# Loading the first 256 tokens by tile, f32 transposes of the first x, and mask constants ahead of GpSimd's loads in a fused attention and gated-MLP kernel

## Chip, cores and metric

The kernel runs on 1 core of one Trainium2 chip. The metric is the device time of one execution in microseconds (us). Before the change it is 263.32 us, the median of three runs.

## What is computed

Attention over 4 batches, 8 heads, 768 tokens and head width 64, followed by a gated MLP with a gated residual. Heads 0, 2 and 6 are causal; the other five see only the first 4 tokens and a window of 64.

```python
scores = where(mask, q @ k.T / 8, -1e9)          # per batch and head
a = softmax(scores)                              # mask: causal, or causal & (sink | window)
x = (a @ v) -> [3072, 512]                       # heads side by side
ffn = (gelu(x @ w_gate) * (x @ w_val)) @ w_out   # d_ff = 1536
out = x + sigmoid(x @ w_res) * ffn               # float32
```

## The kernel before

The 3072 tokens are cut into six chunks of 512 tokens (`CHUNKS`), that is four tiles of 128. For each chunk the kernel computes attention for four pairs of heads (`PAIRS`: 0 and 2, 4 and 6, 1 and 3, 5 and 7), and then the MLP. Chunk 0 is computed in two halves of two tiles, here called first and second half, so that its first gate and value products (`g0` to `g3`, `v0` to `v3`, `L1135`) can start on the first half.

Every operation is a task of a graph. Nothing is scheduled while the program is built. `PLAN` is a list of task numbers written out by hand (a `w` entry puts that many matmuls on a blank tile on TensorE as fillers, and a suffix such as `a` or `d` picks ScalarE or VectorE for a task that may run on several engines). Each engine runs its tasks strictly in the order of the list. `PLACES` gives the buffer for each allocation. `assign_waits` adds the semaphore waits that the dependencies need. A task number is its position in the order of construction, so any added or removed task renumbers the list.

The steps that the change and the prediction touch:

- `loads_first` (`L640`) loads the first 256 tokens of queries and keys of batch 0 as f32: four transfers on the SP queue for keys and four on the ACT queue for queries, one per pair of heads (`ldf`, `L651`). Each is followed by a cast to f16 on VectorE, ScalarE or GpSimd (`c16`, `L657`, `L658`), by transposes on TensorE (`qkT`, `L666`) and by a copy out of PSUM (`qkE`, `L676`). The transposed keys and queries are `kT` and `qT`. The staging buffers come from `P_st` (three of them) and the f16 copies from `P_x16`.
- The remaining loads are issued by GpSimd (`dma`, `L538`), which casts to f16 on the way: queries and keys in `loads_rows` (transposed at `L723`, copied out at `L734`), values in `values`, and weights in `load_weights`. GpSimd also builds the identity and the masks (`L512` to `L525`, tasks named `const`); in `PLAN` these stand between its first loads.
- `scores` (`L892`) multiplies keys by queries, the exponentials follow on ScalarE (`L908`, `L912`), and the masks are applied on VectorE (`L944`). `sink_scores` (`L983`) does the four sink tokens.
- `weigh` multiplies by the values (`win`, `av`, `avk`), takes the reciprocal of the sums (`L1070`), and writes x twice in chunk 0: as f16 for the transposes (`norm16`, `L1081`) and as f32 for the residual (`norm`, `L1083`).
- `to_features` transposes the f16 x on TensorE (`xT`, `L1105`) and copies it out of PSUM (`xE`, `L1113`).
- `gate_value` does the gate and value products, the gelu (`L1140`, `L1171`) and their product (`L1143`, `L1173`). Exponentials and gelu need different activation tables on ScalarE.

In `mm` (`L473`) a matmul may be issued as one full product (`L476`) or as two products of 64 columns of the array (`L477`), whichever tiling TensorE is in when the task comes up.

Of the kernel before, what the change touches and what calls it, by code (L numbers as in the profile page):

```python
# [4 lines left out]
NHEAD = 8  # L5
# [8 lines left out]
NPAIR = NHEAD // 2  # L14
# [415 lines left out]
def build_kernel(nc, q, k, v, w_gate, w_val, w_out, w_res, out):  # L430
# [105 lines left out]
    def dma(eng, prio, cost, out_ap, in_ap, bufs=(), deps=(), name="ld", grp=None):  # L536
        issue = 0.85 if eng == "pool" else 1.2
        return G.add(eng, issue, lambda e: e.dma_start(out_ap(), in_ap), deps, prio, bufs=bufs, dma=cost, name=name, grp=grp)  # L538
# [1016 lines left out]
```

## Time and profile before

| what | value |
|---|---|
| median of three runs | 263.32 us (262.81 to 264.11) |
| the profiled execution | 263.6 us, span 261.9 us |
| TensorE clock granted, mean | 1.000 |
| TensorE busy | 251.9 us, 96% of the span |
| VectorE busy | 206.2 us, 79% |
| ScalarE busy | 159.1 us, 61% |
| GpSimd busy | 104.3 us, 40% |
| moved by DMA | 33.70 MB, mean 129 GB/s |

The profile describes one execution. Its engines are PE (TensorE matmul), PEld (TensorE weight load, beside PE), DVE (VectorE), ACT (ScalarE), POOL (GpSimd) and SP (SyncE). A group row names line, engine, operation, output and inputs, shapes and count, then busy time in us and the mean ns of one, and behind the bar the engine's idle time ahead of it with what ended it. A row of the timeline begins with start and length in us. The chain of waits is followed backwards from the last instruction, at each step to what released it.

### The profile page before, as it was taken

The numbers are of one execution on the slowest core, as the hardware profiler recorded it, in microseconds if no ns is written. First come the engines' busy times: TensorE is split into PE (matmuls) and PEld (weight loads), VectorE is DVE, ScalarE is ACT, GpSimd is POOL, SyncE is SP. The second block draws the span as 40 slices with busy tenths as digits, with TensorE's granted clock in tenths as the row PEclk, the third lists the DMA queues.
The fourth block names the chain that finished last, engine by engine and source line by source line (L and its number), as shares of the span: only waits on it lengthen the run. The fifth ranks groups of instructions, "written<-read, shape, count | busy, mean of one in ns | idle before, by whom it ended". The sixth has DMA issues, their size and how long they took to land.

```text
span 261.9 us, 8050 instructions
## 1 busy us (share of the span) xinstructions
PE 251.9 (96%) x3404; PEld 179.7 (69%) x3404; DVE 206.2 (79%) x472; ACT 159.1 (61%) x282; POOL 104.3 (40%) x142
## 2 busy tenths in 40 slices
PE   6899999999999999999999999999999999999992
PEld 4467754457567667666687567689678678987891
DVE  3599645799879898498998587999587898577975
ACT  2489535867574997245894347884546994555420
POOL 8699952505809906168371563002201010110031
PEclk9999999999999999999999999999999999999999
DMA  6999999996999997999998799609975017230013
GB/s 152 175 175 206 195 202 192 195 148 104 151 174 207 217 120 116 141 205 162 164 103 119 107 149 261 95 3 93 247 105 82 4 12 113 36 49 3 0 36 130
DMA packets 102131, 33.70 MB, mean 129 GB/s; under 512 B 86736, under 2 KB 97232, under 8 KB 102096
## 3 DMA queue, kind: packets, MB, share of 16 engines
q0 software_dynamic: 72592, 18.36, 79.2%
q1 hardware_dynamic: 27840, 13.52, 25.5%
q10 hardware_dynamic: 1664, 1.31, 1.5%
q8 instruction: 27, 0.44, 0.8%
q14 instruction: 8, 0.07, 0.1%
HBM read 29.36 MB, written 10.49 MB: 152 GB/s over the span
## 4 chain that ended last, share of the span: by engine, by line
PE 88%; DVE 7%; DMA 2%; issue 1%; ACTq 1%; ACT 0%; DVEq 0%
PE ps L476 47%; PE ps L477 31%; PE ps L892 5%; DMA qks<-in_q_dram 2%; PE ps L1105 1%; PE ps L1016 1%; DVE x L1081 1%; PE ps L983 1%; DVE xtok L1083 1%; PE ps L1456 1%; ACTq L651 1%; DVE otile L1397 1%; DVE hT L1270 0%; DVE kT L734 0%; PE ps L666 0%
## 5 line engine op out<-in xcount | busy, mean ns | idle before, releaser
L1401 POOL DMA_DIRECT2D out_dram<-otile x16 | 14.5, 904 | 95.7 <-DVE otile L1397 63.5
L476 PE MATMUL ps<-xT,wg 128*128 128x512 f16 (+1 forms) x172 | 38.5, 337 | 0.4 <-DVE x L1081 0.4
L476 PE MATMUL ps<-xT,wv 128*128 128x512 f16 (+1 forms) x168 | 37.5, 339 | 0.0
L1171 ACT ACTIVATE gact<-ps 128x512 f16<-128x512 f32 x38 | 21.8, 596 | 23.6 <-PE ps L476 13.8
L1173 DVE SCALAR_TENSOR_TENSOR hT<-gact,ps 128x512 f16<-128x512 f16 x38 | 26.0, 683 | 11.4 <-PE ps L476 4.9
L538 POOL DMA_DIRECT2D qks<-in_k_dram x35 | 28.8, 842 | 15.1 <-PE ps L723 8.2
L538 POOL DMA_DIRECT2D qks<-in_q_dram x35 | 30.2, 902 | 7.8 <-DMA qT<-qks 7.8
L1245 DVE TENSOR_TENSOR ps<-ps,otile 128x256 f32<-128x256 f32 x60 | 24.3, 428 | 8.9 <-PE ps L477 4.1
L538 POOL DMA_DIRECT2D va<-in_v_dram x24 | 24.3, 1021 | 12.4 <-PE ps L476 12.4
L476 PEld LDWEIGHTS ps<-xT,wv 128*128 128x128 f16 x168 | 16.1, 98 | 11.2 <-ACT gact L1263 0.2
L476 PEld LDWEIGHTS ps<-xT,wg 128*128 128x128 f16 x172 | 16.3, 98 | 10.1 <-DVE x L1081 0.7
L1263 ACT ACTIVATE gact<-ps 128x512 f16<-128x512 f32 x30 | 16.7, 597 | 10.7 <-PE ps L477 5.5
L908 ACT ACTIVATE ea<-ps 128x1024 f16<-128x1024 f32 (+2 forms) x24 | 21.5, 923 | 1.4 <-PE ps L892 1.4
L1270 DVE SCALAR_TENSOR_TENSOR hT<-gact,ps 128x512 f16<-128x512 f16 x30 | 19.5, 683 | 2.2 <-PE ps L476 1.2
L1341 ACT ACTIVATE srs<-ps 128x512 f32<-128x512 f32 x22 | 12.9, 599 | 12.3 <-PE ps L477 8.6
L1241 ACT ACTIVATE ps<-ps 128x256 f32<-128x256 f32 x25 | 9.3, 371 | 16.2 <-PE ps L476 11.8
L1373 DVE TENSOR_TENSOR otile<-otile,ps 128x256 f32<-128x256 f32 x33 | 13.7, 418 | 6.5 <-PE ps L477 4.3
L477 PE MATMUL ps<-xT,wv 128*64 128x512 f16 (+1 forms) x152 | 18.5, 340 | 0.0
L476 PE MATMUL ps<-wo,hT 128*128 128x256 f16 (+1 forms) x114 | 18.2, 295 | 0.0
L477 PE MATMUL ps<-xT,wg 128*64 128x512 f16 (+1 forms) x144 | 17.9, 344 | 0.0
L892 PE MATMUL ps<-qT,kT 64*128 64x64 f16 (+4 forms) x391 | 17.1, 216 | 0.8 <-DVE kT L734 0.5
L1083 DVE TENSOR_TENSOR xtok<-ps,rcp 128x512 f32<-128x512 f32 (+1 forms) x28 | 17.0, 610 | 0.5
(182 smaller groups left out, 594.5 us busy)
## 6 DMA issues: line engine op xcount, KB each, us to landing
out_dram<-xtok SPq DMA_DIRECT2D x4, 1024.0 KB, 6.2
out_dram<-otile POOLq DMA_DIRECT2D x16, 256.0 KB, 4.3
va<-in_v_dram POOLq DMA_DIRECT2D x24, 128.0 KB, 8.2
qks<-in_q_dram POOLq DMA_DIRECT2D x32, 64.0 KB, 7.3
qks<-in_k_dram POOLq DMA_DIRECT2D x32, 64.0 KB, 7.4
wg<-in_moe_w_gate_dram POOLq DMA_DIRECT2D x3, 512.0 KB, 10.6
wv<-in_moe_w_val_dram POOLq DMA_DIRECT2D x3, 512.0 KB, 12.4
wo<-in_moe_w_out_dram POOLq DMA_DIRECT2D x4, 384.0 KB, 21.5
```

Of the source, the lines that this page charges most:

```text
L476: return e.matmul(o, lhsT=lhsT, rhs=rhs, **k)
L477: return [e.matmul(o[h:h + 64], lhsT=lhsT[:, h:h + 64], rhs=rhs, **k) for h in (0, 64)][-1]
L538: return G.add(eng, issue, lambda e: e.dma_start(out_ap(), in_ap), deps, prio, bufs=bufs, dma=cost, name=name, grp=grp)
L892: return [e.matmul(at(scr)[:, oo:oo + w], lhsT=side(BB, qb, low, 1)[half, k0:k0 + 128], rhs=side(BB, qb, low, 0)[half, qq:qq + w], start=T ...
L908: return e.activation(out=o, in_=i_, func=AF.Exp, scale=SM_SCALE)
L1083: t2 = G.add("dve", c_dve(2 * n * 64), lambda e: e.tensor_tensor(out=xview(), in0=avv(0, DHEAD), in1=scale(), op=ALU.mult), [t1] + xdeps, ...
L1171: ta = G.add("act", c_act(512), (lambda gb=gb, ga=ga, gw=gw: lambda e: e.activation(out=at(ga)[:, :], in_=at(gb)[:, gw], func=AF.Gelu))(), ...
L1173: th = G.add("dve", c_dve(512), (lambda vb=vb, ga=ga, f=f, vw=vw: lambda e: e.scalar_tensor_tensor(out=hv(f), in0=at(ga)[:, :], scalar=0.5 ...
L1245: return G.add("dve", c_dve(256), lambda e: e.tensor_tensor(out=at(ps)[:, o], in0=at(ps)[:, BL], in1=at(es)[:, 0:256], op=ALU.add), deps, ...
L1263: ta = G.add("act", c_act(512), (lambda x=x, ga=ga, both=both: lambda e: e.activation(out=two(at(ga)[:, :]), in_=both(x), func=AF.Gelu))() ...
L1270: th = G.add("dve", c_dve(512), (lambda x=x, f=f, ga=ga, both=both: lambda e: e.scalar_tensor_tensor(out=two(hv(f)), in0=two(at(ga)[:, :]) ...
L1401: t = G.add("pool", 1.0, (lambda ot=ot, r0=r0: lambda e: e.dma_start(out[r0:r0 + 128, :], at(ot)[:, :], accum_op=ALU.add))(), ends + [stor ...
```

## The change

- `loads_first` issues two transfers per hardware queue instead of four. Each covers all eight heads of one tile of 128 tokens. The eight casts now belong to halves of a tile (four heads each), and each of the four transpose groups takes one tile of keys or queries with all pairs. The copy out of PSUM writes consecutive tokens.
- In the first half of chunk 0, x is no longer written as f16. The transposes read the f32 x with an f32 identity, `ident32`, which is kept in `xs3` until that buffer's own first use. The copy out of PSUM reads f32 there.
- In the second half of chunk 0, heads 0, 2 and 4, 6 write the f32 x first and cast it to f16 from there; in the new list the cast is on GpSimd. The other two pairs write f16 and f32 as before.
- Every GpSimd load depends on all of GpSimd's constant tasks.
- Copies of the window mask may run on ScalarE too.
- `PLAN` and `PLACES` are replaced for the whole kernel. In the new list the load of ScalarE's exponential table stands right behind its two transfers, there are 33 fillers instead of 42, and one exponential of chunk 1 stands between gelus of chunk 0.

```diff
+    ident32 = xs3[:, 0, :].bitcast(FP32)
...
+    t_ident32 = G.flex({"dve": (0.2, lambda e: e.tensor_copy(out=ident32[:, :], in_=ident[:, :])),
+                        "act": (0.3, lambda e: e.activation(out=ident32[:, :], in_=ident[:, :], func=AF.Copy))}, [t_ident], -58, name="ident")
+    xs3_last = [t_ident32]
...
-        return G.add(eng, issue, lambda e: e.dma_start(out_ap(), in_ap), deps, prio, bufs=bufs, dma=cost, name=name, grp=grp)
+        return G.add(eng, issue, lambda e: e.dma_start(out_ap(), in_ap), list(deps) + (consts if eng == "pool" else []), prio,
+                     bufs=bufs, dma=cost, name=name, grp=grp)
...
+    consts = [x for x in G.tasks if x.name == "const"]
...
-        for p in ORDER:
-            h = PAIRS[p][0]
+        for i in range(2):
             for j, src, eng in ((1, k, "sp"), (0, q, "act")):
-                    view(j, p).rearrange("p (x w) -> p x w", x=2),
-                    src[b, h:h + 3:2, lo:lo + 256, :].rearrange("x (p i) d -> p x (i d)", i=2)))(),
-                    [], -60, bufs=[st[j]], dma=0.5, name="ldf")
+                    view(j, i, 0, 2).rearrange("p (h d) -> p h d", h=NHEAD),
+                    src[b, :, lo + 128 * i:lo + 128 * i + 128, :].rearrange("h p d -> p h d")))(),
+                    [], -60, bufs=[st[j]], dma=0.9, name="ldf")
+                for o in range(2):
...
-        for k_ in (0, 2):
-            ps_ = sorted(ORDER[k_:k_ + 2])
+        for i in range(2):
             for j in (1, 0):
...
-                x16 = Buf(P_x16)
+                x16 = None if c == 0 and l0 == 0 else Buf(P_x16)
...
-        direct = c == 0 or heads[0] % 2
+        direct = x16 is not None and heads[0] % 2
...
-        if not direct:
+        if x16 is None:
+            xdeps.append(t2)
+        elif not direct:
...
+            on = ("dve", "act") if c else ("dve", "act", "pool")
...
+        plain = x16 is None
+        view = (lambda s: at(s)) if plain else at16
...
+            out=at(scr)[:, i * 128:(i + 1) * 128], in_=at(xbuf)[:, l0 + i, cb * 128:(cb + 1) * 128], identity=ident32[:, :])
```

More of the change, by code (lines that the diff above doesn't have):

```diff
@@ L525, in build_kernel @@
         (64, aff(m_win[:, 2, 0:64], ALU.is_ge, 0.0, 0, [[1, 64]], -1))])
-    t_win0 = [spread(("dve",), -50, m_win[:, 3:5, :], m_win[:, 1:2, :].to_broadcast([128, 2, 128]), 256, t_win)]
-    t_win = t_win0 + [spread(("dve",), 600, m_win[:, 5:7, :], m_win[:, 1:2, :].to_broadcast([128, 2, 128]), 256, t_win),
-                      spread(("dve",), 600, m_win[:, 0, :], m_win[:, 1, :], 128, t_win)]
+    t_win0 = [spread(("dve", "act"), -50, m_win[:, 3:5, :], m_win[:, 1:2, :].to_broadcast([128, 2, 128]), 256, t_win)]
+    t_win = t_win0 + [spread(("dve", "act"), 600, m_win[:, 5:7, :], m_win[:, 1:2, :].to_broadcast([128, 2, 128]), 256, t_win),
+                      spread(("dve", "act"), 600, m_win[:, 0, :], m_win[:, 1, :], 128, t_win)]
     for i, vk in enumerate(P_vk.items):
@@ L645, in loads_first @@
         st, half = [Buf(P_st), Buf(P_st)], [Buf(P_x16), Buf(P_x16)]
-        view = lambda j, p: at(st[j])[:, :].bitcast(FP32)[:, p * 256:(p + 1) * 256]
-        h16 = lambda j, p: at(half[j]).rearrange("p c i k -> p (c i k)")[:, p * 256:(p + 1) * 256]
-        for p in ORDER:
-            h = PAIRS[p][0]
+        view = lambda j, i, o, n=1: at(st[j])[:, :].bitcast(FP32)[:, (i * 2 + o) * 256:(i * 2 + o + n) * 256]
+        h16 = lambda j, i, o, n=1: at(half[j]).rearrange("p c i k -> p (c i k)")[:, (i * 2 + o) * 256:(i * 2 + o + n) * 256]
@@ L650, in loads_first @@
+        for i in range(2):
             for j, src, eng in ((1, k, "sp"), (0, q, "act")):
-                ld = G.add(eng, 0.6, (lambda src=src, j=j, p=p, h=h: lambda e: e.dma_start(
-                    view(j, p).rearrange("p (x w) -> p x w", x=2),
-                    src[b, h:h + 3:2, lo:lo + 256, :].rearrange("x (p i) d -> p x (i d)", i=2)))(),
-                    [], -60, bufs=[st[j]], dma=0.5, name="ldf")
-                def cast(on, j=j, p=p):
-                    return lambda e: (e.activation(out=h16(j, p), in_=view(j, p), func=AF.Copy) if on == "act" else
-                                      e.tensor_copy(out=h16(j, p), in_=view(j, p)))
@@ L659, in loads_first @@
-                tok[j, p] = G.flex({e: (0.4, cast(e)) for e in ("dve", "act", "pool")}, [ld], -205, bufs=[st[j], half[j]], name="c16")
-        for k_ in (0, 2):
-            ps_ = sorted(ORDER[k_:k_ + 2])
+                ld = G.add(eng, 0.6, (lambda src=src, j=j, i=i: lambda e: e.dma_start(
+                    view(j, i, 0, 2).rearrange("p (h d) -> p h d", h=NHEAD),
+                    src[b, :, lo + 128 * i:lo + 128 * i + 128, :].rearrange("h p d -> p h d")))(),
+                    [], -60, bufs=[st[j]], dma=0.9, name="ldf")
@@ L662, in loads_first, with cast @@
+                for o in range(2):
+                    def cast(on, j=j, o=o, i=i):
+                        return lambda e: (e.activation(out=h16(j, i, o), in_=view(j, i, o), func=AF.Copy) if on == "act" else
+                                          e.tensor_copy(out=h16(j, i, o), in_=view(j, i, o)))
+                    tok[j, i, o] = G.flex({e: (0.4, cast(e)) for e in ("dve", "act", "pool")}, [ld], -205, bufs=[st[j], half[j]], name="c16")
+        for i in range(2):
             for j in (1, 0):
@@ L663, in loads_first @@
                 scr = Buf(P_ps, "scr0")
-                to, o0 = (BB.kt, lo) if j else (qb, qo)
-                tt = G.add("pe", 0.3, (lambda scr=scr, j=j, ps_=ps_: lambda e: [
-                    e.transpose(out=at16(scr)[64 * x:64 * x + 64, (m * 2 + i) * 128:(m * 2 + i + 1) * 128],
-                                in_=h16(j, p)[:, x * 128 + i * 64:x * 128 + i * 64 + 64], identity=ident[:, :])
-                    for m, p in enumerate(ps_) for i in range(2) for x in range(2)])(),
-                    [t_ident] + [tok[j, p] for p in ps_], 40 * k_ - 205, bufs=[half[j], scr], name="qkT")
+                to, o0 = (BB.kt, lo + 128 * i) if j else (qb, qo + 128 * i)
@@ L670, in loads_first, with ev @@
+                tt = G.add("pe", 0.3, (lambda scr=scr, j=j, i=i: lambda e: [
+                    e.transpose(out=at16(scr)[64 * x:64 * x + 64, p * 128:(p + 1) * 128],
+                                in_=h16(j, i, 0, 2)[:, PAIRS[p][x] * 64:PAIRS[p][x] * 64 + 64], identity=ident[:, :])
+                    for p in range(NPAIR) for x in range(2)])(),
+                    [t_ident] + [tok[j, i, o] for o in range(2)], 80 * i - 205, bufs=[half[j], scr], name="qkT")
                 tt.mode = "col"
-                def ev(on, scr=scr, to=to, o0=o0, ps_=ps_):
+                def ev(on, scr=scr, to=to, o0=o0):
@@ L673, in fn @@
                     def fn(e):
-                        o = at(to)[:, ps_[0]:ps_[1] + 1:ps_[1] - ps_[0], o0:o0 + 256].rearrange("c m (p i) -> c m p i", i=2)
-                        i_ = at16(scr)[:, 0:512].rearrange("c (m i p) -> c m p i", m=2, i=2)
+                        o = at(to)[:, :, o0:o0 + 128]
+                        i_ = at16(scr)[:, 0:512].rearrange("c (m w) -> c m w", m=NPAIR)
                         return e.tensor_copy(out=o, in_=i_) if on == "dve" else e.activation(out=o, in_=i_, func=AF.Copy)
@@ L677, in ev @@
                     return fn
-                t = G.flex({"dve": (c_dve(512), ev("dve")), "act": (c_act(512), ev("act"))}, [tt], 40 * k_ - 205,
+                t = G.flex({"dve": (c_dve(512), ev("dve")), "act": (c_act(512), ev("act"))}, [tt], 80 * i - 205,
                            bufs=[scr, to], name="qkE")
-                for p in ps_:
-                    for i in range(a, a + 2):
-                        (BB.ktok if j else BB.qtok)[p, i] = t
+                for p in range(NPAIR):
+                    (BB.ktok if j else BB.qtok)[p, a + i] = t
@@ L852, in attention @@
                   for cb in (P.heads[0] // 2, P.heads[1] // 2):
-                    to_features(c, cb, P.pr, x16, xdeps, xtbuf, xttoks, l0, len(tiles))
+                    to_features(c, cb, P.pr, x16, xdeps, xtbuf, xttoks, l0, len(tiles), xbuf)
         return last
@@ L1090, in cast @@
                                   e.tensor_copy(out=at(x16)[:, :, 0:n, half], in_=xview()))
-            xdeps.append(G.flex({"dve": (0.57, cast("dve")), "act": (c_act(n * 128), cast("act"))},
+            on = ("dve", "act") if c else ("dve", "act", "pool")
+            xdeps.append(G.flex({e: (0.57 if e == "dve" else c_act(n * 128), cast(e)) for e in on},
                                 [t2], pr + 122, bufs=[xbuf, x16], name="x16"))
@@ L1101, in to_features_dma, with to_features @@
         xttoks += [(cb, t), (cb + 1, t)]
-    def to_features(c, cb, pr, x16, xdeps, xtbuf, xttoks, l0, n):
+    def to_features(c, cb, pr, x16, xdeps, xtbuf, xttoks, l0, n, xbuf):
         scr = Buf(P_ps, "scr")
-        tp = G.add("pe", c_mm(128, n), lambda e: [e.transpose(
+        plain = x16 is None
+        view = (lambda s: at(s)) if plain else at16
+        tp = G.add("pe", c_mm(128, n), (lambda e: [e.transpose(
+            out=at(scr)[:, i * 128:(i + 1) * 128], in_=at(xbuf)[:, l0 + i, cb * 128:(cb + 1) * 128], identity=ident32[:, :])
+            for i in range(n)]) if plain else lambda e: [e.transpose(
             out=at16(scr)[h:h + w, i * 128:(i + 1) * 128], in_=at(x16)[:, cb % 2, i, h:h + w], identity=ident[:, :])
             for i in range(n) for h, w in (((0, 64), (64, 64)) if G.run == "col" else ((0, 128),))],
-            xdeps + [t_ident], pr - 3, bufs=[x16, scr], name="xT")
+            xdeps + [t_ident32 if plain else t_ident], pr - 3, bufs=[xbuf if plain else x16, scr], name="xT")
         ph(c, "xT").append(tp)
+        if plain:
+            xs3_last.append(tp)
         def ev(on):
             def fn(e):
-                o, i_ = at(xtbuf)[:, cb, l0 * 128:(l0 + n) * 128], at16(scr)[:, 0:n * 128]
+                o, i_ = at(xtbuf)[:, cb, l0 * 128:(l0 + n) * 128], view(scr)[:, 0:n * 128]
                 return e.activation(out=o, in_=i_, func=AF.Copy) if on == "act" else e.tensor_copy(out=o, in_=i_)
@@ L1276, in fast @@
         toks[FA:] = toks[FA::2] + toks[FA + 1::2]
-    gvtok, gas, gv_tail, xs3_last = {}, {}, [], []
+    gvtok, gas, gv_tail = {}, {}, []
     def sums(c, h, htoks, pa=0):
```

152 rows, old and new, of tables (PLACES, PLAN) are left out of this document.

## The prediction

> **What bounds the kernel now.** I read the page first, then the chain of waits in order of time, then busy time by stretch, then the rows of the first 30 us. The page:
>
> ```profile
> span 261.9 us, 8050 instructions
> PE 251.9 (96%) x3404; PEld 179.7 (69%) x3404; DVE 206.2 (79%) x472; ACT 159.1 (61%) x282; POOL 104.3 (40%) x142
> PE 88%; DVE 7%; DMA 2%; issue 1%; ACTq 1%; ACT 0%; DVEq 0%
> ```
>
> TensorE is busy throughout, but the 96% hold fillers on `blank`. The chain (start, length, what) shows where PE truly is the bound:
>
> ```profile
> 2.39 6.09 DMA qks<-in_q_dram
> 8.50 0.30 DVE x L658
> 8.85 1.07 PE ps L666 x16
> ...
> 20.89 0.03 issue
> ...
> 26.53 0.43 DVE x L1081
> ...
> 27.64 0.22 PE ps L1105 x4
> 27.87 15.63 PE ps L476 x96
> ...
> 258.40 0.69 DVE otile L1407
> ```
>
> The last query transfer holds the start until 8.50, VectorE and its neighbours until 26.96, and from 27.87 the matrix engine. What reaches 27.87 earlier moves everything behind it. Busy time in those stretches (length; PE, PEld, DVE, ACT, POOL; clock; DMA share; GB/s):
>
> ```profile
> 11.90:27.10 15.20, 13.91 (x269) 9.86 (x268) 13.21 (x43) 13.79 (x26) 15.03 (x22) 1.00 1.47 191
> 27.80:43.50 15.70, 15.70 (x100) 9.13 (x99) 7.50 (x19) 6.65 (x14) 8.48 (x11) 1.00 1.55 194
> 43.50:204.00 160.50, 160.50 (x2008) 111.42 (x2010) 135.24 (x298) 104.46 (x183) 64.02 (x81) 1.00 1.28 144
> ```
>
> In the first row DVE (13.21) and ACT (13.79 of 15.20) are both nearly full. In the others PE never pauses and both have room.
>
> **The change, part by part.** The two transfers per hardware queue carry the same 1.05 MB, but in pieces of one 64-value row (256 B, 4,096 of them) instead of two rows (512 B, 2,048). The rows are: 3.0 to 4.5 us, hardware transfers almost alone; then 9 to 12 us, GpSimd's transfers alone, all small.
>
> ```profile
> DMA packets 863, 0.41 MB, mean 276 GB/s; under 512 B 55, under 2 KB 863, under 8 KB 863
> q0 software_dynamic: 3, 0.00, 0.5%
> DMA packets 2937, 0.49 MB, mean 163 GB/s; under 512 B 2937, under 2 KB 2937, under 8 KB 2937
> ```
>
> The first is 575 packets per us, the second 979. No row has 256-byte packets on the hardware queues. Bounds, from data beginning at 2.39: unchanged bytes per us (276 GB/s) 3.8 us, so 6.2; 979 packets per us 4.2 us, so 6.6; 575 packets per us 7.1 us, so 9.5. I take 979, whose packets are small as the new ones are, and 0.3 us to be seen: last arrival 6.9 against 8.50.
>
> The Trainium skill ("DMA: Bandwidth & Descriptors", Specifications) says transfers below 512 B miss line rate; its section "Why small descriptors are slow" counts 3 extra cycles per packet, 11 for 256 B and 19 for 512 B, so 1.16 times the time per byte. That estimate would put the arrival at 6.8; the bare rule alone speaks against this change, and no run here has shown either.
>
> That nothing else is on the DMA engines meanwhile comes from the constants. GpSimd now does all nine before its first load. In 0 to 12 us it was busy 9.17, of which its DMA issues were 6.75:
>
> ```profile
> 0.00:12.00 12.00, 6.75 (x8) 1.00 1.26 162
> sum 12.00, PE 8.64 PEld 5.38 DVE 5.90 ACT 3.41 POOL 9.17; mean PE 8.64 PEld 5.38 DVE 5.90 ACT 3.41 POOL 9.17
> 1.67 1.11 POOL L538 DMA_DIRECT2D qks<-in_q_dram  x1
> 9.26 0.88 POOL L538 DMA_DIRECT2D qks<-in_k_dram  x1 [2.08 <-DVE x L658]
> 14.63 0.75 POOL L538 DMA_DIRECT2D wg<-in_moe_w_gate_dram  x1
> 24.48 0.61 PE L476 MATMUL ps<-xT,wg 128*128 128x256 f16 x4
> ```
>
> So the constants cost at most 2.4 us: the first load goes from 1.67 to about 3.2. Three packets by 4.5 us say that its data began some 1.7 us after its issue ended at 2.78; now that is about 6.0, when the hardware transfers are nearly done. The later loads wait for nothing that was early. In the new order the first gate weights are GpSimd's eighth load (tenth before), after seven issues of about 0.9 from 3.2, so near 9.5 instead of 14.63, while their first user ran at 24.48. The rows of chunk 1 that are put behind the weights are first needed after 43 us (the chain's piece from 27.87 ends at 43.50, in front of their transposes). Cover gone, each load would cost its issue, 0.9.
>
> From arrival to scores: ACT's table load leaves the path (its new place is ahead of the data).
>
> ```profile
> 2.91 1.28 ACT L657 ACT_TABLE_LOAD   x1 [2.91 <-issue]
> L657 ACT ACTIVATE x<-qks 128x256 f16<-128x256 f32 x2 | 0.8, 416 | 1.2 <-DMA qks<-in_k_dram 1.2
> L676 DVE COPY qT<-ps 128x512 f16<-128x512 f16 x2 | 1.4, 692 | 0.8 <-PE ps L666 0.8
> 11.25 0.40 PE L892 MATMUL ps<-qT,kT 64*128 64x64 f16 x8
> 14.22 0.41 PE L723 MATMUL ps<-ident,qks 128*64 128x128 f16 x8
> ```
>
> It gains nothing on the path, because the last arrival was later. Three ACT casts of 0.42 now follow the last arrival in a row: 6.9 to 8.2; transposes (half of L666's 1.07) 8.7; two evictions of 0.69 on DVE behind each other, partly overlapped: scores at 9.9. By tile, every score needs all four transfers, where pair 0 used to start after half; that early start is lost (the chain does not pass through it). Two score groups and a transpose group (0.40, as much, and 0.41) precede DVE's next eviction: 11.1.
>
> DVE's stretch from there to the last f16 write of x that the transposes wait for, by kinds:
>
> ```profile
> L1081 DVE TENSOR_TENSOR x<-ps,rcp 128x256 f16<-128x256 f32 x8 | 3.3, 420 | 0.1
> L1070 DVE RECIPROCAL rcp<-ps 128x4 f32<-128x4 f32 x8 | 1.4, 175 | 0.0
> L734 DVE COPY kT<-ps 128x512 f16<-128x512 f16 x2 | 1.3, 662 | 0.0
> L734 ACT ACTIVATE qT<-ps 128x1024 f16<-128x1024 f16 x1 | 1.0, 1005 | 0.0
> L1113 ACT ACTIVATE xT<-ps 128x256 f16<-128x256 f16 x1 | 0.4, 377 | 0.0
> L616 DVE COPY vs<-va 64x455 f16<-64x455 f16 (+1 forms) x2 | 1.0, 476 | 0.1
> sum 15.20, DVE 3.65; mean DVE 3.65
> ```
>
> The last row is the ten masks alone. New list: 3 evictions 2.0, masks 3.65, 3 value copies 1.4, 8 reciprocals 1.4, 8 x writes at 0.42 3.4, one x eviction from f32 0.42 (as a 256-wide f32 read), one 1024-wide eviction of chunk 1 that ACT did before 1.3: 13.6 in 34 instructions, with 0.03 between two (as the chain's issue piece at 20.89): 14.6, so 25.7. Six f16 writes of x are gone (2.5), but a 1024-wide eviction, a value copy and one f32 write moved in, so DVE's stretch barely shrinks; it was 11.93 to 26.96. ACT gives up two 1024-wide evictions (1.0 each) and takes 7 instead of 2 x evictions (0.38 each), so it stays beside DVE.
>
> Second half: heads 0, 2 and 4, 6 get their f16 x by a GpSimd cast, behind the residual weights' issue. GpSimd's nearest prices are 0.43 (a 128x256 f16 select) and 0.86 (L1407, 128x256 f32 add).
>
> ```profile
> L496 POOL TENSOR_SCALAR_AFFINE_SELECT m_win<-m_win 128x256 f16<-128x256 f16 x2 | 0.9, 430 | 0.1
> L1407 POOL TENSOR_TENSOR otile<-otile,xtok x4: 722/861/1265, 252.7 to 256.2; 128x256 f32<-128x256 f32 x3, 128x512 f32<-128x512 f32 x1
> L1105 PE MATMUL ps<-ident,x 128*128 128x128 f16 x12 | 1.3, 219 | 0.2 <-DVE xtok L1083 0.2
> L1456 PE MATMUL ps<-blank 128*128 128x256 f16 x25 | 4.7, 326 | 0.0
> 29.04 1.48 PE L476 MATMUL ps<-xT,wg 128*128 128x256 f16 x12
> ```
>
> The second cast may start at about 25.2 and, at 0.6, ends at 25.8, level with DVE; at 0.86 it costs 0.3 to 0.5. Queued behind it are one chunk-1 load and the output weights: no one needs them before 43 us. So the last two transposes run at 25.8 and end at 26.2 (0.39 as at 27.48), against 27.87: 1.7 earlier. By then PE has also done one more value group (4 matmuls, (1.48-0.27)/11 = 0.11 each): 0.44.
>
> f32 transposes: eight of the first half, 0.10 apart as f16 (0.40 for four). No row has one. Bounds: 0, or four times, 8 x 0.30 = 2.4 us, cushioned by fillers (4.7 us of them in the first row's stretch, about half left now). I take 0.4 on the path, nearer the free end because PE waits for DVE there.
>
> Later stages: the new order has PE change its tiling 61 times behind this point, 63 before; one exp stands between gelus in chunk 0, two more table loads in ACT's 9 us of slack (27.8 to 43.5). Taken as nothing; without that cover 2 x 1.28. The tail keeps its order but for two output issues that go from ACT's queue to SP's. Spreads and initial fills that move between engines: nothing, they lie in idle time.
>
> Sum on the profiled execution: 1.7 + 0.44 - 0.4 = 1.7. It took 263.6 (span 261.9), 0.3 over the median 263.32. 263.3 - 1.7 = 261.6.
>
> **The rivals.**
> 1. Small packets hold the start: 575 packets per us, last arrival 9.5 or later, since GpSimd's data then shares the engines from 6.0. Everything shifts by 2.6 against the sum: 263.3 - 1.7 + 2.6, 264.2, and with half of it 262.9. For: 256 B is new on these queues; against: 979 per us of GpSimd's small ones. By the skill's bare 512 B rule this is what happens.
> 2. The change does not do what it says for the end: DVE's stretch hardly shrinks, so with f32 transposes at four times, half covered (1.2 instead of the 0.4 taken), and the cast at 0.86 (0.4) the gain is 1.7 - 0.8 - 0.4 = 0.5: 262.8, no change. For: DVE and ACT both full in the first row. Against: fillers.
> 3. Slower: exp between the gelus. ACT then spends 1.28 + 0.6 + 1.28 = 3.2 in which no gate bank is freed, and PE runs out of PSUM banks. It decides once over 1.7 of the 3.2 is uncovered; wholly uncovered, 263.3 - 1.7 + 3.2 = 264.8. Against: ACT's 6.65 busy of 15.70, and PE has other banks for some 2 us.
>
> **How the numbers follow.** 0.5%, 1.3 us, is about what a measurement tells from no change. My forecast (faster, own range 260.2 to 262.0) 0.55; rivals 1 and 2 0.15 each, mostly within 0.5%; rival 3 or rival 1 at its worst 0.15. Faster 0.57, same 0.28, slower 0.15. The range reaches from arrival at 6.2 with free f32 transposes and 0.8 more found in the order (259.8) to rival 1 at its end (264.2).
>
> **What would show it.** Last first-stage cast before 8.5; scores near 9.9; gate matmuls continuous from about 26; no GpSimd packet before 5 us. Wrong if the last arrival is past 8.5, if the f32 transposes stand over 0.2 apart with PE waited for, if PE pauses between 27 and 35 us, or if the stretch behind it grows.

## The result, and the profile after

The changed kernel takes 260.44 us (median; 260.23 to 261.0), the kernel before in the same series 263.29. The ratio is 0.989, with an interval from 0.986 to 0.992: faster by about 2.85 us, where 1.7 were forecast. The profiled execution took 261.0 us, its span is 259.3. It is the longest of the four; the others took 260.23 to 260.50.

From the page of the changed kernel, the span, the busy times and the shares of the chain of waits:

```profile
span 259.3 us, 8020 instructions
PE 250.1 (96%) x3393; PEld 176.1 (68%) x3393; DVE 203.0 (78%) x453; ACT 164.9 (64%) x298; POOL 105.1 (41%) x144
PE 93%; DVE 2%; DMA 2%; ACT 1%; issue 1%; DVEq 0%
```

The chain had 7% on VectorE and now has 2%. Its rows in order of time (start, length, what):

```profile
0.81 4.67 DMA qks<-in_q_dram
...
5.50 0.46 DVE x L663
...
6.01 0.49 DVE vk L535
...
8.95 0.61 ACT kT L680
...
11.47 0.65 PE ps L895 x13
...
20.02 0.96 ACT vs L622
...
25.57 0.45 PE ps L1115 x8
...
27.23 17.85 PE ps L477 x100
...
255.71 0.69 DVE otile L1419
```

The chain leaves the transfers at 5.5, with the first query tile, and not at 8.50 with the last queries; but scores (L895) run at 11.4. Before, a first group ran at 7.3 and the next at 11.25. From there the chain goes through TensorE and a few ScalarE pieces around 20 us. Between 7.7 and 252 us it has no piece of VectorE, which it followed up to 26.96 before. Busy time in the stretches shown of before (length; PE, PEld, DVE, ACT, POOL; clock; DMA share; GB/s):

```profile
11.90:27.10 15.20, 14.55 (x259) 10.48 (x254) 12.52 (x37) 13.63 (x30) 9.84 (x17) 1.00 1.39 200
27.80:43.50 15.70, 15.70 (x90) 8.53 (x89) 5.80 (x12) 9.68 (x17) 6.32 (x8) 1.00 1.50 196
43.50:204.00 160.50, 160.50 (x2068) 111.19 (x2068) 135.15 (x293) 109.92 (x193) 70.73 (x89) 1.00 1.32 143
```

In the first row VectorE has six instructions fewer (37 for 43) and GpSimd 5.2 us less. In the other two TensorE is full, as before, but it gets through the rest sooner. To see this, I count from the last x transposes of each chunk and add up the planner's own costs of the TensorE work that the list still holds behind that place ("left"). At equal work left, the changed kernel is ahead by 1.35 us at the end of chunk 0's first stage, by 1.3 to 1.4 after chunks 1 to 3, by 1.7 after chunk 4, 2.6 after chunk 5, and 2.7 at the end. By this count half of the gain is in the first 26 us and half comes later. The costs are the planner's estimates, and the first figure is not exact: with the same start, `a_then_b` below ran those transposes at 24.6 in its profiled execution and not at 25.4, because TensorE worked at half rate for a shorter time there (last section).

### The profile page after: what moved, and what is told of

Same layout as the page of the kernel before. It is cut to its first block, busy times and chain, and to the rows that moved or that the text cites. A ratio compares the mean times of both kernels' runs of the same rounds, so it can differ in the third digit from the quotient of the medians.

```text
span 259.3 us, 8020 instructions
## 1 busy us (share of the span) xinstructions
PE 250.1 (96%) x3393; PEld 176.1 (68%) x3393; DVE 203.0 (78%) x453; ACT 164.9 (64%) x298; POOL 105.1 (41%) x144
## 4 chain that ended last, share of the span: by engine, by line
PE 93%; DVE 2%; DMA 2%; ACT 1%; issue 1%; DVEq 0%
PE ps L477 49%; PE ps L478 31%; PE ps L895 6%; DMA qks<-in_q_dram 2%; PE ps L1019 2%; PE ps L726 1%; PE ps L1115 1%; PE ps L1468 1%; PE ps L986 1%; PE ps L670 1%; DVE otile L1409 1%; DVE x L663 0%; DVE vk L535 0%; ACT vs L622 0%; ACT es L911 0%
## 5 line engine op out<-in xcount | busy, mean ns | idle before, releaser
L1413 POOL DMA_DIRECT2D out_dram<-otile x16 | 15.4, 995 | 84.9 <-DVE otile L1409 54.7
L542 POOL DMA_DIRECT2D qks<-in_q_dram x35 | 32.5, 950 | 17.5 <-issue 8.6
L542 POOL DMA_DIRECT2D qks<-in_k_dram x35 | 32.8, 973 | 12.8 <-PE ps L726 12.8
L1257 DVE TENSOR_TENSOR ps<-ps,otile 128x256 f32<-128x256 f32 x60 | 24.9, 431 | 9.8 <-PE ps L478 5.1
L542 POOL DMA_DIRECT2D va<-in_v_dram x24 | 24.1, 1035 | 5.1 <-PE ps L477 5.1
L1353 ACT ACTIVATE srs<-ps 128x512 f32<-128x512 f32 x22 | 13.1, 596 | 15.3 <-PE ps L478 11.6
L478 PE MATMUL ps<-xT,wv 128*64 128x512 f16 (+1 forms) x156 | 19.2, 341 | 0.0
L895 PE MATMUL ps<-qT,kT 64*128 64x64 f16 (+3 forms) x391 | 16.9, 216 | 0.6 <-ACT xT L1125 0.6
L478 PE MATMUL ps<-xT,wg 128*64 128x512 f16 (+1 forms) x144 | 17.3, 344 | 0.0
```

What stands on the lines that cost most here:

```text
L478: return [e.matmul(o[h:h + 64], lhsT=lhsT[:, h:h + 64], rhs=rhs, **k) for h in (0, 64)][-1]
L895: return [e.matmul(at(scr)[:, oo:oo + w], lhsT=side(BB, qb, low, 1)[half, k0:k0 + 128], rhs=side(BB, qb, low, 0)[half, qq:qq + w], start=T ...
L1257: return G.add("dve", c_dve(256), lambda e: e.tensor_tensor(out=at(ps)[:, o], in0=at(ps)[:, BL], in1=at(es)[:, 0:256], op=ALU.add), deps, ...
L1413: t = G.add("pool", 1.0, (lambda ot=ot, r0=r0: lambda e: e.dma_start(out[r0:r0 + 128, :], at(ot)[:, :], accum_op=ALU.add))(), ends + [stor ...
```

## The experiments

Two theories. A: the gain is the start's, from the earlier arrival, as the prediction has it. B: half belongs to the order of the later list. Further: which of the start's edits is it? All ratios are against the kernel before, run beside each kernel (its medians 263.16 to 263.53).

| kernel | median, us | ratio, interval |
|---|---|---|
| a_then_b | 264.99 | 1.007, 1.005 to 1.009 |
| b_then_a | 265.71 | 1.009, 1.006 to 1.012 |
| a_vzero | 259.44 | 0.986, 0.984 to 0.988 |
| a_nofill | 261.38 | 0.993, 0.991 to 0.996 |
| after_again | 260.24 | 0.989, 0.986 to 0.991 |
| a_between | 259.82 | 0.987, 0.984 to 0.989 |
| a_f16x | 262.63 | 0.997, 0.994 to 1.000 |
| a_both | 259.52 | 0.986, 0.983 to 0.988 |
| a_loads8 | 260.56 | 0.990, 0.988 to 0.993 |
| a_best | 259.60 | 0.986, 0.982 to 0.989 |
| a_late_b | 266.57 | 1.014, 1.010 to 1.018 |
| a_row512 | 260.68 | 0.991, 0.989 to 0.994 |

**Start and later order apart: a_then_b and b_then_a.**

```diff
a_then_b (changed kernel's code)
-PLAN = after
+PLAN = after[:245] + (the rest, in the order of before)
b_then_a (code of before)
-PLAN = before
+PLAN = before[:285] + (the rest, in the order of after)
```

> The changed kernel's start (its list up to the end of chunk 0's attention, about 27 us) followed by the old order for everything behind it. Theory: of the 2.8 us gained, the start gave 1.35 (equal TensorE work is reached that much earlier at 27 us) and the later order 1.3. Then this runs at 263.3 - 1.35 = 261.9. Rival: the whole gain comes from the start; then 260.5, as the changed kernel. A third reading, all from the later order: 263.3.

> The mirror: the old start up to the end of chunk 0's attention, then the changed kernel's order. Theory (1.35 from the start, 1.3 from the later order): 263.3 - 1.3 = 262.0. Rival (all from the start): 263.3. Third reading (all from the later order): 260.5.

Both totals are slower than either parent, and no theory's number was met: each seam makes stalls of its own. The chain of a_then_b and then that of b_then_a, near the seam:

```profile
47.14 0.60 ACT srs L1440
47.75 1.28 ACT L912
49.05 1.02 ACT ea L912
50.07 0.60 ACT ek L994
```

```profile
42.01 1.08 ACT gact L1172 x2
...
43.76 1.28 ACT L1459
45.06 0.21 ACT scratch L1459
45.26 0.92 ACT ea L909
```

ScalarE gets table loads and exponentials in front of what TensorE waits for. Behind the seam the two can still be used. Time from chunk 1's last x transposes to the last VectorE addition, and planned TensorE work left at the first:

| | list behind | from, to | time | work left | over the plan |
|---|---|---|---|---|---|
| before | old | 67.6, 258.4 | 190.8 | 181.55 | 9.25 |
| a_then_b | old | 68.0, 259.3 | 191.3 | 181.55 | 9.75 |
| after | new | 65.3, 255.7 | 190.4 | 182.41 | 8.0 |
| b_then_a | new | 70.2, 260.7 | 190.5 | 182.41 | 8.1 |

The new list takes 1.2 to 1.7 us less for the same work, with either start. In plain time it is 0.4 to 0.8; the other 0.86 is the planner's price for the work that the new list still has left there. Part of it shows in the trace. What TensorE waited for between 67 and 257 us, in the kernel before:

```profile
PE ps L477 <- issue: 0.4, 1, 0.4
PE ps L892 <- DVE hT L1270: 0.3, 1, 0.3
```

a_then_b has the wait for hT again (0.3), another of 0.4 for a transfer and one of 0.2, which may be the joint's; the changed kernel and b_then_a have none. Output matmuls in half tiles from 67 us on (groups by line: count | busy, mean ns | idle), in before and after:

```profile
L477 PE MATMUL ps<-wo,hT 128*64 128x256 f16 x216 | 15.5, 274 | 0.4 <-issue 0.4
```
```profile
L478 PE MATMUL ps<-wo,hT 128*64 128x256 f16 x216 | 14.7, 274 | 0.0
```

The same 216 matmuls take 0.8 us less; in a_then_b and b_then_a they take 15.2 and 14.6. Not every group gains: the value products in half tiles take 13.6 us for 96 before and 14.5 for 100 after. So B holds for about half of the gain by the planner's sums, and not by the totals of the two spliced kernels. Which exchange in the list does it is not shown.

**Where in the later list: a_late_b.**

```diff
-PLAN = after
+PLAN = after[:1248] + (the rest, in the order of before)
```

> The changed kernel up to its 1,248th place of the order (about 181 us, just behind the last x transposes of chunk 4), then the rest in the order of the kernel before. Theory 'most of what the later order gained lies in chunks 4 and 5': behind that point the kernel before took 74.6 us for 71.5 of planned TensorE work and the changed kernel 73.8 for 71.7, so the time rises by about 1.0, to 261.2 (ratio 0.992), with TensorE pauses of 0.3 each near 205 and 221 as in the kernel before. Rival 'the gain is spread over all chunks or belongs to the start': it rises by less than 0.4, to at most 260.7 (0.990). The seam itself may add up to some tenths, which would show as a pause right behind 181 us.

This one tells nothing on the question. It is 6.3 us slower, and its chain shows a mishap of the joint:

```profile
214.33 4.32 DMA out_dram<-otile
218.67 0.44 DVE otile L1380
219.15 3.05 PE ps L479 x50
```

An output tile is needed again before its transfer to memory is through, so TensorE stands for 2.8 us. The place of the later gain inside the list stays open.

**The two memsets: a_vzero.** VectorE clears the sink values (L535) between two first casts, from 6.01 to 7.05.

```diff
 PLAN = "0 17 18 214 217 211 1 220 199 212a 216 6 7
-15 218a 16 2 215 ... 9 10 222 5 227 221a 228 229 230 11 12 232
+218a 2 215 ... 9 10 222 5 227 221a 228 229 230 11 12 15 16 232
```

> The changed kernel with VectorE's two initial fills of vk (0.49 us each, now between its first and second cast) moved behind its last eviction of the first 256 tokens, where it idles 1.7 us. Theory: they lie on the chain to the first scores, so scores start 1.0 us earlier (10.4 instead of 11.40) and the kernel takes 259.5 to 260.0 instead of 260.5. Rival: the last key transfer, first cast at 7.25, and the five fillers set the first scores anyway; then no change, 260.5.

It is 0.8 to 1.0 us faster than the changed kernel. In its trace the memsets stand behind the evictions, the first scores come 0.9 earlier, and the second half's x transposes start at 24.1 instead of 25.4. Part of these 1.3 us is not the edit's: TensorE worked at half rate until about 11.6 us in this execution and until about 13.9 in the changed kernel's. a_best below, with the same memsets and half rate until about 13.8, has the transposes at 24.8:

```profile
10.01 1.04 DVE L536 MEMSET vk<- 128x520 f16 x2
10.47 0.45 PEld L896 LDWEIGHTS ps<-qT,kT 64*128 64x128 f16 x15 [0.41 <-issue]
```

**The idle matmuls: a_nofill and a_both.**

```diff
 PLAN = "... 215 8 w20 225 219a ...
-... 224a w5 420 ... w3 431 ... w2 467 ... w3 440 ...
+... 224a 420 ... 431 ... 467 ... 440 ...
(a_both: this and the edit of a_vzero)
```

> The changed kernel without the 13 fillers behind the first transposes (the first 20 stay). Theory: the five ahead of the first scores and the eight later ones stand on TensorE's own chain (1.18, 0.61, 0.33 and 0.43 us pieces of it), and about 0.6 us of that comes back: 259.9. Rival A: they only fill waits, 260.5. Rival B: without them the granted clock falls in this stretch, and it is slower, over 261.

> The changed kernel with the two memsets of the sink values moved behind the last eviction of the first queries and without the thirteen idle matmuls on the blank tile that stand in TensorE's queue after the first loads. With the memsets moved alone the kernel took 259.4 us, without the idle matmuls alone 261.4. Theory 'the five idle matmuls before the first scores now delay them' (they ended at 10.5 where the last eviction had ended at 9.8): first scores at 9.9 instead of 10.5, last transposes of x near 23.6, time near 258.9 (ratio 0.984). Rival 'the idle matmuls pay for themselves, whatever they cost at the start': about 0.9 above the kernel with the memsets moved, as between the other two, 260.3 (ratio 0.989).

Without the 13 later ones the changed kernel takes 0.9 us more (the intervals just overlap), yet with the memsets moved it makes no difference (259.52 and 259.44). a_both starts its scores at 10.00 instead of 10.47 and ends the first stage no earlier (x transposes at 24.0, against 24.1). Neither theory of a_both met its number. a_nofill's 261.38 lies where rival B put it. Its granted clock speaks against B: 0.999 in the profiled execution, and 0.997 in a run of 262.2 against 0.980 in one of 260.4. The matmuls of the profiled execution speak for B. The same six scores in a_nofill and in the changed kernel:

```profile
16.31 0.60 PE L895 MATMUL ps<-qT,kT 64*128 64x128 f16 x6
```
```profile
16.41 0.39 PE L895 MATMUL ps<-qT,kT 64*128 64x128 f16 x6
```

In a_nofill TensorE works at half rate until about 19 us, in the changed kernel and in a_both until about 13.9, all with a recorded clock of 1.00. Whether the missing idle matmuls bring this, and whether it makes the 0.9 in the other runs, is not shown: a_both lacks them too.

**The constants: a_between.**

```diff
-list(deps) + (consts if eng == "pool" else [])
+list(deps)
 PLAN: "4 232 231 233 234 236 235 5", GpSimd's loads, back between the constants as in before
```

> The changed kernel with GpSimd's constants put back between its first loads, in the order in which the kernel before had them, and nothing else of the change undone. Theory 'constants ahead made the start earlier': GpSimd's transfers then share the engines with the first loads of queries and keys from about 3 us on, the last of these lands near 8.3 instead of about 7.0, the last first-stage cast ends near 10 instead of 9.5, and the time rises by about 0.9 to 1.3 us to 261.3 to 261.7 (ratio 0.993 to 0.994). Rival 'the arrival did not decide, VectorE's queue behind it did' (two memsets of 0.49 us and the casts): the last load lands later but the last cast does not move by more than 0.3, and the time stays within 0.4 of 260.4 (0.988 to 0.991).

Neither number is met. The load does not land later, which the rival had expected too, and the time falls by 0.4 us (within the intervals), just below the rival's range. GpSimd's first load is issued at 1.69, as in before:

```profile
1.69 1.10 POOL L543 DMA_DIRECT2D qks<-in_q_dram  x1
...
7.18 1.38 ACT L663 ACTIVATE x<-qks 128x256 f16<-128x256 f32 x4 [3.60 <-DMA qks<-in_k_dram]
...
8.84 0.28 DVE L664 CAST x<-qks 128x256 f16<-128x256 f32 x1
```

The keys' second transfer still lands at 7.1. The last first-stage cast ends at 9.1, earlier than the changed kernel's 9.5. GpSimd's packets do not come before 6 us here either. So with two long transfers on each hardware queue the place of the constants does not move the arrival.

**What moved the arrival: a_loads8 and a_row512.** First four transfers of half the heads, then two transfers with 512-byte pieces:

```diff
a_loads8
+                for o in range(2):
-                    view(j, i, 0, 2).rearrange("p (h d) -> p h d", h=NHEAD),
-                    src[b, :, lo + 128 * i:lo + 128 * i + 128, :].rearrange("h p d -> p h d")
+                        view(j, i, o).rearrange("p (h d) -> p h d", h=NHEAD // 2),
+                        src[b, 4 * o:4 * o + 4, lo + 128 * i:lo + 128 * i + 128, :].rearrange("h p d -> p h d")
a_row512
-                    src[b, :, lo + 128 * i:lo + 128 * i + 128, :].rearrange("h p d -> p h d")
+                    src[b, 4 * i:4 * i + 4, lo:lo + 256, :].rearrange("h (p t) d -> p h (t d)", t=2)
```

> The changed kernel with each of its four first loads split in two by heads (heads 0 to 3, heads 4 to 7), so four transfers of 128 KB on each hardware queue as in the kernel before, still in 256-byte pieces; each cast waits for its own half. Nothing else differs. Theory 'two long transfers per queue keep the queue full, and this, not the constants, moved the last arrival from 8.5 to 7.0': the hardware queues pause near 4 to 5 us as in the kernel before (167 GB/s there against 245), GpSimd's packets get in before 6 us, the last load lands at about 8 and the time rises by 0.5 to 1.3, to 260.8 to 261.5 (ratio 0.991 to 0.993). Rival 'the number of transfers is nothing': last arrival within 0.3 of 7.0, the first casts start earlier since they wait for half a transfer, time 259.6 to 260.4 (0.986 to 0.989).

> The changed kernel with its two first transfers per hardware queue cut by heads (0 to 3, then 4 to 7) over all 256 tokens, two tokens to a partition, so in pieces of 512 bytes as in the kernel before instead of 256; casts, turns and evictions follow the new places, with evictions that write in steps of two elements. Order, constants and everything behind it are the changed kernel's. The last arrival was 8.5 with four transfers of 512-byte pieces, 7.0 with two or with four of 256-byte pieces. Theory 'the kernel before emptied its queues': its first two transfers per queue (0.52 MB) were through at 4.0 us, before the third was ready, and GpSimd's packets got in; with two long transfers the queues stay full, 512-byte pieces move at 276 to 312 GB/s, and the last load lands between 5.9 and 6.6. Rival 'the 512-byte layout itself is what was slow': last arrival near 8 or later, GpSimd's packets before 6 us. For the time both add two evictions of 0.69 instead of 0.42 us on VectorE: with the arrival at 6.3, 260.0 to 260.6 (ratio 0.987 to 0.990); with 8.5, 261.0 to 262.0 (0.992 to 0.995).

The transfers by second. Before, 4 to 5 us, with its queues; then 4 to 5 us of after and of a_loads8; then 3 to 4 and 4 to 5 us of a_row512, and 3 to 4 of after:

```profile
DMA packets 366, 0.17 MB, mean 167 GB/s; under 512 B 62, under 2 KB 366, under 8 KB 366
...
q0 software_dynamic: 43, 0.01, 15.6%
```
```profile
DMA packets 976, 0.25 MB, mean 245 GB/s; under 512 B 976, under 2 KB 976, under 8 KB 976
```
```profile
DMA packets 850, 0.21 MB, mean 212 GB/s; under 512 B 850, under 2 KB 850, under 8 KB 850
```
```profile
DMA packets 691, 0.35 MB, mean 346 GB/s; under 512 B 16, under 2 KB 691, under 8 KB 691
```
```profile
DMA packets 629, 0.31 MB, mean 313 GB/s; under 512 B 17, under 2 KB 629, under 8 KB 629
```
```profile
DMA packets 1105, 0.28 MB, mean 280 GB/s; under 512 B 1105, under 2 KB 1105, under 8 KB 1105
```

In a_loads8 the last load lands as in the changed kernel (no hardware packet after 7 us), so the number of transfers by itself is nothing and that theory fell. In a_row512 ScalarE's casts start at 6.26, near a microsecond earlier, so 512-byte pieces are not slow in themselves. The kernel before had three things together: 512-byte pieces, four short transfers on a queue, and GpSimd's loads from 1.67 us on. There 0.22 MB moved from 2 to 3 us and 0.31 from 3 to 4, which is as much as the first two transfers of each queue hold (0.52 MB). Then the rate fell, and GpSimd's packets got in. In the changed kernel, a_between, a_loads8 and a_row512 more than 200 GB/s go on from 3 to 6 us. Each of the three things alone, put back into the changed kernel, leaves the arrival at about 7 us or earlier, so at least two of them were needed. Which two is not shown; that short, fast transfers were through before the next were ready is a guess. By 256-byte pieces the same bytes take 1.24 (346 to 280) and 1.28 times (313 to 245) as long.

Nevertheless the time is the same in all three (260.24, 260.56 and 260.68), though the first scores of the profiled executions come at 11.40, 10.83 and 10.27. Arrivals between 6.1 and 7.0 do not decide by themselves; a_row512 also pays 0.67 to 0.69 instead of 0.41 to 0.43 us for each of VectorE's first three copies out of PSUM. No run has an arrival of 8.5 with the rest of the change.

**x in f32: a_f16x.**

```diff
-                x16 = None if c == 0 and l0 == 0 else Buf(P_x16)
+                x16 = Buf(P_x16)
-        direct = x16 is not None and heads[0] % 2
+        direct = (c == 0 and l0 == 0) or heads[0] % 2
```

> The changed kernel with the first half's x written as float16 again beside the float32 copy and turned as float16, and nothing else undone. This gives back four multiplications of even heads into the float16 tile and takes the eight float32 transposes away. Theory 'the float32 turn saved VectorE's time on the path': the stretch from 11.9 to 27.1 us, where VectorE was busy 12.4 of 15.2 us, gets four operations of about 0.43 us more, the last transposes of x move from 25.4-26.0 to about 26.2-26.8, and the time rises by 0.7 to 1.0 us to about 261.3 (ratio 0.992). Rival 'VectorE has room there, since ScalarE's exponentials and the TensorE decide': last transposes within 0.2 of 25.4, time within 0.3 of 260.4 (0.988 to 0.990).

The first theory holds in kind; its 0.7 to 1.0 was too small. The twelve runs go from 261.36 to 264.85, nearly in step with the mean granted clock: 0.989 to 0.991 in the five lowest (261.4 to 261.7), 0.969 in the three highest (264.1 to 264.9); one of 263.0 has 0.991. So four more VectorE writes, with the f32 transposes gone, cost 1.1 to 1.5 us. Where TensorE's longer pauses bring the clock down once more, about 2.7 come on top (spans 262.4 and 259.7). The profiled run is one with 0.969; its stretches (columns as above, clock third from the end):

```profile
19.50:21.00 1.50, 0.69 (x16) 0.55 (x16) 1.47 (x6) 1.48 (x3) 0.00 (x0) 0.95 1.25 207
21.00:22.50 1.50, 1.29 (x11) 0.80 (x13) 1.47 (x7) 1.13 (x4) 0.00 (x0) 0.50 1.24 205
...
25.50:27.00 1.50, 1.50 (x18) 1.17 (x16) 0.92 (x4) 0.38 (x1) 0.14 (x1) 0.50 1.24 206
```

VectorE is busy 1.47 of 1.50 there while TensorE stands; then TensorE works at half clock on its gates. The last x transposes run at 28.5.

**Both good edits: a_best.**

```diff
 the edits of a_between and of a_vzero together
```

> The changed kernel with both edits that helped: GpSimd's constants between its first loads, and the two memsets of the sink values behind the last eviction of the first queries. Each alone brought the last transposes of x from 25.4 to 24.1. Theory 'both edits end at the same floor, which ScalarE and VectorE set between 13 and 24 us (each busy over 13 of 15.2)': transposes again at 24.1, time 259.4 to 259.9 (ratio 0.985 to 0.987). Rival 'they take time from different waits and add up': transposes at 23.2 or before, time 258.7 or less (0.983).

259.60: they do not add up. The floor theory's time is met; the transposes stood at 24.8 in its profiled run, the longest of five, so their place was not. a_vzero, a_both and a_best are equal within their intervals. a_vzero is the simplest of them and the best version that came out of this, 0.8 to 1.0 us below the changed kernel by medians; the intervals of the two just overlap.

## Why the prediction was right, and where it was not

The direction, the rejected rivals and the range were right. The two halves of the sum were not what they were said to be, and that the time fell into the range is in part luck: the start gave less than was forecast, and a term that was taken as nothing gave as much. Of the four signs named ahead, two came: TensorE runs without a pause from 25.85 on, and no GpSimd packet moves before 5 us. The last first-stage cast ended at 9.5 and not before 8.5, and the scores were late.

**Arrival 6.9: near; its worth: not shown.** The last data came at 7.0, and ScalarE was released at 7.25. The constants ahead, which the step counted on, did nothing (a_between). The 1.7 us from GpSimd's issue to its first packet was no fixed delay: in a_between it is more than 3 us. And the row that gave 276 GB/s runs into the slow stretch shown above (334 to 344 GB/s up to 3.75 us, 188 to 230 behind it), so it was no rate of 512-byte pieces. The Trainium skill ("DMA: Bandwidth & Descriptors", Why small descriptors are slow) gave an estimate of 1.16 times the time per byte; the runs show 1.24 and 1.28, so its direction holds, in the arrival though not in the time.

**Scores at 9.9: the step that failed.** They came at 11.40. Rows of the changed kernel:

```profile
7.25 1.33 ACT L662 ACTIVATE x<-qks 128x256 f16<-128x256 f32 x4 [3.65 <-DMA qks<-in_k_dram]
...
8.86 0.64 DVE L663 CAST x<-qks 128x256 f16<-128x256 f32 x1
...
10.22 1.25 PE L1468 MATMUL ps<-blank 128*128 128x256 f16 x5
...
11.40 0.72 PE L895 MATMUL ps<-qT,kT 64*128 64x64 f16 x15
```

The step priced three ScalarE casts behind the arrival. The chain runs elsewhere: through VectorE's two memsets (6.01 to 7.05) and the cast behind them, transposes at half rate (7.84 to 9.33), a copy on ScalarE (8.95 to 9.55), the last transposes, and five idle matmuls in front of the scores. VectorE's last cast, behind an eviction, ends at 9.5, level with that copy.

**VectorE's stretch of 14.6, "barely shrinks": wrong by two microseconds.** It ran from 12.73 to 25.38, so 12.65, and held the 34 instructions that were listed. Three value copies took 1.0 and not 1.4. The rest is that the instructions overlap:

```profile
17.57 0.42 DVE L1086 TENSOR_TENSOR xtok<-ps,rcp 128x256 f32<-128x256 f32 x1
17.91 0.17 DVE L1073 RECIPROCAL rcp<-ps 128x4 f32<-128x4 f32 x1
18.11 0.42 DVE L1086 TENSOR_TENSOR xtok<-ps,rcp 128x256 f32<-128x256 f32 x1
```

A write of 0.42 is followed 0.34 later; the prediction added 0.03 to full durations in 34 instructions where about 0.06 to 0.08 goes off most of them. This error and the one before cancelled, by luck: the last x transposes were forecast to end at 26.2 and ended at 26.0. With scores no earlier than before, the start's gain was made in this stretch. a_f16x puts a price on it: the dropped f16 writes are worth 1.1 to 1.5, as much as all of the start's 1.35. What the late arrival would have cost beside them is not shown.

**f32 transposes, 0.4: mis-sized.** They stood 0.13 apart, against 0.10 for f16, so 0.2 for eight, and nothing waited for them:

```profile
L1113 PE MATMUL ps<-xs,xtok x8: 272/273/329, 19.6 to 20.5; 128*128 128x128 f32 x8
```

**GpSimd's casts at 0.6: mis-sized.** Two took 0.74 from 24.57 and ended at 25.31, in front of VectorE.

**Later order "taken as nothing": the term missing from the sum.** By the planner's sums it brought 1.2 to 1.7 us. The argument from the number of tiling changes (61 for 63) looked at the wrong thing: waits (0.7 in all) and spaces between output matmuls went. The start's 1.35 and about 1.3 of this term make the 2.7 of the traces; the medians have 2.85.

**Rival 1** (small packets) fell: the pieces are slower, but the last arrival was 7.0 and not 9.5. **Rival 2** fell with the f32 price. **Rival 3** fell: the two more table loads at 29.4 and 31.7 are there, and TensorE shows no pause between 27 and 43.5.

## What to carry to other kernels

An earlier arrival is worth only what the queues behind it let through: read each engine's list up to the first result, idle work and initial clears included, before moving the load. Price a full engine by start-to-start distances, not by durations. When an order written out by hand is replaced as a whole, the stages behind the edit are a term of their own: set the time at equal work left beside the old order's, chunk by chunk; splicing two orders measures the joint as much as the halves. Before two traces are compared, compare the time that the same matmuls take in both, and not the recorded clock alone.

## What the runs showed of the hardware

TensorE worked at half rate for some microseconds behind its first pause, and a recorded clock of 1.00 did not exclude it. The same stretch in the first and in the repeated profile of the changed kernel (clock third from the end):

```profile
12.00:13.50 1.50, 1.50 (x26) 1.09 (x24) 0.77 (x2) 1.09 (x3) 1.36 (x4) 1.00 2.25 161
```
```profile
12.00:13.50 1.50, 1.50 (x26) 1.09 (x24) 0.77 (x2) 1.09 (x3) 1.36 (x4) 0.50 2.26 162
```

The matmuls took the same time in both. Two groups of sixteen transposes in the first, then the earlier of the two in the repeat:

```profile
12.05 1.06 PE L726 MATMUL ps<-ident,qks 128*64 128x128 f16 x16
...
14.31 0.64 PE L726 MATMUL ps<-ident,qks 128*64 128x128 f16 x16
```
```profile
12.05 1.07 PE L726 MATMUL ps<-ident,qks 128*64 128x128 f16 x16
```

The half rate follows a pause of 2.27 us in the first and of 2.96 in the repeat, and lasts to about 13.9 and 14.2 us; the span is 259.3 in both. The kernel before has it too, with a recorded clock of 1.000: sixteen transposes take 1.07 at 8.85 us and 0.64 at 13.00. In a_then_b, with the changed kernel's start, it ends near 11.3, and the second half's x transposes come 0.8 earlier. So a difference of up to 0.8 us between two single traces need not be the edit's. In a_f16x a second fall at 21 us, where TensorE is needed, cost up to 2.7. The Trainium skill ("TensorE: Matmul & The Clock Gate", What's actually happening) states a half clock after an idle window of about 3.4 us that runs freely; the pauses here were a little shorter, and that the half rate ends at different times with the same list agrees with the free-running window.

VectorE's cast of the same 128x256 tile took 0.22 to 0.28 us in some places and 0.64 to 0.73 in others; the long ones of the changed kernel and of a_between all lay beside a load being issued by GpSimd, though some short ones did too. The Trainium skill ("SBUF — State Buffer", SBUF: two separate sides) has the two engines share a pair of ports, on which one can block the other; no run here separates that from other causes.
